# A feed-forward kernel whose next tile's token blocks are prepared at an even pace over a tile's quartets, in a fixed order behind TensorE's products

## The chip, the cores and the metric

One Trainium2 chip, one core. The metric is the device time of one execution in microseconds (us). Engines: PE is TensorE (matrix products), DVE is VectorE, ACT is ScalarE, POOL is GpSimd, SP issues the transfers (DMA).

## What is computed

Attention with 32 landmarks (Nyström) over 4 batches of 576 tokens, and behind it two feed-forward networks over all 2304 tokens (model width 512, inner width 2048). The change lies in the second network. Cut to that:

```python
x = attn_out.transpose(0, 2, 1, 3).reshape(B * S, H * D)      # 2304 x 512
x = _moe_ref(x, w_in, w_out)                                  # first network: x1d in the kernel
h = x @ w_in                                                  # second: 512 -> 2048
g = np.where(h > 0.0, h, np.exp(np.minimum(h, 0.0)) - 1.0)    # ELU
return (g @ w_out).astype(np.float32)                         # 2048 -> 512
```

## The kernel before

The first network leaves its result in DRAM as `x1d`. The second one works on three tiles of 768 tokens (`NTT = 3`), and for each of them on eight quartets (`NQ = 8`) of 256 inner columns. I count the quartets of a tile from 0 to 7. All products are made three times over pairs of numbers, a high part `h` and a low part `l` that together hold a float32 (`wh*xh + wh*xl + wl*xh`).

`quartet(q)` makes the 2x2 block product of weights and tokens by a scheme with seven block products in place of eight (Winograd's form of Strassen's). Each of the seven is a `block`: six matmuls of 128x384 (`h<-x,wi` in the trace) into one of two PSUM banks `h`. So a block can start when the block before the last one has been emptied: the first by ACT's copy `a<-h` (`a1` in the code), the second by DVE's addition `u<-h,a`, the third by `y<-h,a`, and so on. ELU follows on DVE and ACT (`gf<-y`, `gf<-gf,y`), and the result is split into a pair: ACT casts it (`gh<-gf`, `ghl<-gf`), and DVE subtracts (`gl<-gf,gh`, `ghl<-gf,ghl`). Between the blocks PE makes the products of the second layer of an earlier quartet (`x<-w,gh` and the like).

The seven blocks need seven token blocks and seven weight blocks, which are sums of the plain ones:

- `load_in2(q + 1)` loads the next quartet's weights during quartet `q` (`wi<-wi2d`, `u<-wi2d`). In the first tile DVE makes eight additions of 128x128 for them (`u<-u,wi`, `u<-wi,u`), ACT casts (`wi<-wi`, `wi<-u`), POOL subtracts (`wi<-wi`, `wi<-u,wi`), and SP stores the result (`wi2p<-wi`). The two later tiles only load what was stored.
- `load_out2(q)` splits the second layer's weights in the first tile: ACT casts and POOL subtracts (`w<-w`, 128x512).
- `load_x(t, eng)` makes the token blocks of tile `t`, in two halves. A half has four loads from `x1d` (into `xf`, the scratch tiles `f`, and into `x`, the blocks' own places), four subtractions on POOL (`xf<-...`) and seven pairs: a cast on ACT (`x<-x`, `x<-xf`) and a subtraction on POOL. It is a generator: one `next` makes one step, 24 steps for a tile, and a 25th ends it.

For the second and third tile the loop over `q` and `p` (the seven blocks of a quartet) takes one step ahead of each block, from quartet 4 of the tile before (`XPACE = 4`) on:

```python
        if q % NQ == XPACE and q // NQ + 1 < NTT:
            xs = load_x(q // NQ + 1, pool)
...
            gate[0] = chain[0]
            next(xs, None)
            gate[0] = None
```

A scheduler decides the order of instructions in each engine's queue. `wanted(s)` sets their priority, and `after(inst, other)` an order that costs no wait on the chip: `inst` is put in its queue only when `other` has been put in its own. `chain[0]` is the last product written so far. `gated(inst)` puts an instruction behind `gate[0]`. Before, only the loads of `load_x` were gated; subtractions and casts went wherever the scheduler saw room. Once the order is set, each engine works through its own queue in that order and waits only for the data of the instruction at its head.

Of the kernel before, what the change touches and what calls it, by code (L numbers as in the profile page):

```python
# [10 lines left out]
F32 = mybir.dt.float32  # L11
# [20 lines left out]
def nystrom_ffn_kernel(ctx: ExitStack, tc, q, k, v, w_in1, w_out1, w_in2, w_out2, out):  # L32
# [56 lines left out]
    NQ = NKT // 2  # L89
    NTT = NT // (2 * T2)  # L90
# [9 lines left out]
    PRE, NLEAD, EI, EO = 2, 2, 3, 4  # L100
    GATE1, O2, NEW1 = 8, 2, 0
    PACE, NEW, PACE1 = 0.5, -4, 0.2
    XSET, XPACE = 4, 4
    NAT = 25, 28, 31

    strict = [False]
# [17 lines left out]
    def after(inst, other):  # L124

        tc.add_manual_dep(
            inst.ins, other.name, mybir.DependencyInfo(mybir.DependencyClass.NoSync, mybir.DependencyReason.DATA)
        )

    vec, act, pool, pe = InOrder(nc.vector), InOrder(nc.scalar), InOrder(nc.gpsimd), InOrder(nc.tensor)  # L130
    sp = InOrder(nc.sync, False)

    def sub(o, a, b, eng=vec):
        return eng.tensor_tensor(out=o, in0=a, in1=b, op=ALU.subtract)
# [22 lines left out]
    def wanted(s):  # L157
        tc.cur_priority = int(1000 * (s + 100))
# [11 lines left out]
    def gated(inst):  # L170
        if gate[0] is not None:
            after(inst, gate[0])
# [77 lines left out]
    def run(gen):  # L250
        for _ in gen:
            pass
# [55 lines left out]
    def to_pair(f, h, l, eng=vec):  # L308
        act.copy(out=h, in_=f)
        sub(l, f, h.bitcast(F32), eng)  # L310
# [54 lines left out]
    def scratch(n, w):  # L365

        return room().bitcast(F32).rearrange("p n t -> p (n t)")[:, 0:n * w].rearrange("p (a n) -> p a n", a=n)
# [609 lines left out]
    xt_t = {}  # L977

    def x_places(t, n=14):

        for i in range(n):
            if t % 2 == 0:
                x = xp[0].tile([128, 2, T2], F32, name="x2", tag=f"x2{i}")
                yield x[:, 0], x[:, 1]
            elif NS + i < len(PLACES):
                x = wop.tile([128, 2, DM], F32, name="x2", tag=PLACES[NS + i])
                yield x[:, 0, 0:T2], x[:, 1, 0:T2]
            else:
                x = nat.tile([128, G, W], F32, name="x2", tag="nl3")
                yield x[:, 0, 0:T2], x[:, 1, 0:T2]  # L990

    def load_x(t, eng):

        places = x_places(t)
        t0 = 2 * T2 * t
        for kk in range(2):
            x = [next(places) for _ in range(7)]
            h, l = [y[0] for y in x], [y[1] for y in x]

            def pair(i, f):  # L1000
                xt_t[t, kk, i] = h[i].bitcast(F32R), l[i].bitcast(F32R)
                to_pair(f, *xt_t[t, kk, i], eng)

            if t:
                f = [
                    nat.tile([128, G, HALF], F32, name="xf", tag=n).rearrange("p g t -> p (g t)")[:, 0:T2]
                    for n in ("ath0", "ath1", "atl0")
                ]
            else:
                f = scratch(2, T2)  # L1010
                f = [f[:, 0], f[:, 1], scratch(1, T2)[:, 0]]
            for o, r, c in ((f[0], 0, 1), (l[0], 0, 0), (l[2], 1, 1), (l[1], 1, 0)):
                gated(sp.dma_start(out=o, in_=x1d[2 * r + kk, :, t0 + c * T2:t0 + c * T2 + T2]))
            yield
            sub(f[1], f[0], l[0], eng)
            yield
            sub(f[0], l[2], f[0], eng)
            yield
            sub(f[2], l[2], f[1], eng)
            yield  # L1020
            pair(5, f[0])
            yield
            sub(f[0], l[1], f[2], eng)
            yield
            for i, g in ((3, f[1]), (4, f[2]), (6, f[0]), (0, l[0]), (1, l[1]), (2, l[2])):
                pair(i, g)
                yield
# [3 lines left out]
    def bmm(*a):  # L1031

        inst = mm(*a)
        if chain[0] is not None:
            after(inst, chain[0])
        chain[0] = inst.ins
# [12 lines left out]
    def elu(key, src, add, gf=None, split=True):  # L1049

        if gf is None:
            gf = ft.tile([128, T2], F32, name="gf", tag="gf", bufs=2)
        c = stg.tile([128, W], F32, name="y", tag="y", bufs=YB)[:, 0:T2]
        vec.tensor_tensor(out=c, in0=src, in1=add, op=ALU.add)
        act.activation(out=gf, in_=c, func=AF.Relu, scale=-1.0)
        act.activation(out=gf, in_=gf, func=AF.Exp, scale=-1.0)
        vec.scalar_tensor_tensor(out=gf, in0=gf, scalar=-1.0, in1=c, op0=ALU.add, op1=ALU.max)
        if split:
            gt[key] = g_pair()
            to_pair(gf, *gt[key])  # L1060
        return gf
# [4 lines left out]
    def sum_places(t):  # L1066

        places = [y for x in x_places(t + 1, NDEF * NQ // 2) for y in x]
        for r in range(NQ):
            for j in range(NDEF):  # L1070
                sums_t[t * NQ + r, j] = places[NDEF * r + j]

    def quartet(q):

        t = q // NQ
        a1 = nat.tile([128, G, HALF], F32, name="a1", tag="atl1").rearrange("p g t -> p (g t)")[:, 0:T2]
        u2 = scratch(1, T2)[:, 0]
        u3 = ft.tile([128, T2], F32, name="u3", tag="at", bufs=1)

        def block(w, x):  # L1080
            ps = banks["h"].tile([128, 512], F32, name="h", tag="h")[:, 0:T2]
            n = 0
            for kk in range(2):
                wh, wl = wi[q, kk]
                xh, xl = xt_t[t, kk, x]
                for a, b in ((wh, xh), (wh, xl), (wl, xh)):
                    bmm(ps, a[:, w, :], b, n == 0, n == 5)
                    n += 1
            return ps

        def add(o, ps, x):
            vec.tensor_tensor(out=o, in0=ps, in1=x, op=ALU.add)

        act.copy(out=a1, in_=block(0, 0))
        yield
        add(u2, block(5, 4), a1)
        yield
        wino = t in WINO
        if wino:
            if q % NQ == 0:  # L1100
                sum_places(t)
            f = scratch(2, T2)
            f22, f11 = f[:, 0], f[:, 1]
            s1, s2, s3 = (sums_t[q, j] for j in range(NDEF))
        else:
            f22 = f11 = None
        elu((q, 0, 0), block(1, 1), a1, f22)
        yield
        add(u3, block(3, 5), u2)
        yield  # L1110
        ps = block(4, 3)
        elu((q, 1, 1), ps, u3, f11)
        add(u2, ps, u2)
        yield
        f = elu((q, 1, 0), block(2, 6), u3, None, not wino)
        if wino:
            pool.tensor_tensor(out=s1, in0=f22, in1=f, op=ALU.add)
            sub(s2, s1, f11, pool)
            sub(s3, f11, f, pool)
        yield  # L1120
        f = elu((q, 0, 1), block(6, 2), u2)
        if wino:
            sub(f, f, s2)
            gt[q, 4] = g_pair()
            to_pair(f, *gt[q, 4])
        yield
# [283 lines left out]
    for i in range(END, NA):  # L1410
# [3 lines left out]
        if r == 0:  # L1414
# [4 lines left out]
            else:  # L1419
# [3 lines left out]
                x0 = load_x(0, vec)  # L1423
# [19 lines left out]
    def late():  # L1443

        for i in range(NA - DELAY, NA):
            a2 = slot_a2(i, bmm)
            for _ in range(NDM):
                next(a2)
                yield
            run(a2)  # L1450

    def seconds():
        for q in range(NTT * NQ):
            yield from (wino2 if q // NQ in WINO else second)(q)
# [1 line left out]
    flush()  # L1456
    wanted(NA - 6)
    load_in2(1)
    behind, tail, xs, more, n = seconds(), late(), x0, iter(()), 0
    for q in range(NTT * NQ):  # L1460
        wanted(NA + 4 * q - 2)
        if q:
            load_in2(q + 1) if q + 1 < NTT * NQ else None
        if q % NQ == XPACE and q // NQ + 1 < NTT:
            xs = load_x(q // NQ + 1, pool)
        steps_ = quartet(q)
        if q == (WINO[0] - 1) * NQ:
            more = (None for r in range(NQ) for _ in sums_out2(r))
        for p in range(7):
            if p == 2:  # L1470
                load_out2(q)
            wanted(NA + 4 * q + 4 * p / 7 + 4)
            if conv and p % 2 == 0:
                conv.pop(0)()
            if p == 4 and q % NQ == NQ - 2 and q // NQ in WINO:
                load_late2(q // NQ, 0)
                load_late2(q // NQ, 1)
            next(more, None)
            gate[0] = chain[0]
            next(xs, None)  # L1480
            gate[0] = None
            wanted(NA + 4 * q + 4 * p / 7)
            next(steps_)
            for _ in range(2):
                next(tail, None)
            while n < (7 * q + p + 1 - 7 - LAG) * 12 * NS2 // 7:
                next(behind)
                n += 1
        run(steps_)
# [37 lines left out]
```

## Time and profile before

| | |
|---|---|
| median of 3 runs | 826.49 us (822.29 to 826.56) |
| profiled execution | 825.29 us, span 823.5 us, mean granted clock 0.991 |
| PE busy | 783.3 us, 95% of the span |
| DVE, ACT, POOL busy | 545.6, 463.7, 413.2 us |
| second network | from 431.68 us (first `h<-x,wi`) to the end |

Busy times are of one execution. Since PE is busy nearly all the time, a wait of another engine matters only where PE waits for it in turn. Tiles are named without numbers: `x` is a token block (or, as a matmul's output, a PSUM bank), `u` scratch, `w` weights of the second layer.

### The profile page before, as it was taken

The page shows a single profiled execution, that of the slowest core. Times are in us where ns is not written, and L with a number is a line of the kernel's source. Part 1 is how long each engine was busy: PE and PEld are TensorE (multiplying, and loading weights), DVE is VectorE, ACT ScalarE, POOL GpSimd, SP SyncE. Part 2 cuts the span into 40 slices and gives each one's busy share as a digit, 9 for nine tenths or more (in the row PEclk, how much of TensorE's full clock was granted, in tenths as well). Part 3 has the DMA queues.
Part 4 walks back from the last instruction along what each step waited for, and adds up shares of the span by engine and source line. Part 5 has one row for each costly group of instructions (what it writes and reads, how often), then busy time and mean ns, then how long its engine had stood idle before and what let it go on. Part 6 is the DMA issues. An engine that isn't in the chain of part 4 may idle for free.

```text
span 823.5 us, 16234 instructions
## 1 busy us (share of the span) xinstructions
PE 783.3 (95%) x5860; PEld 694.7 (84%) x5860; DVE 545.6 (66%) x1076; ACT 463.7 (56%) x1020; POOL 413.2 (50%) x423
## 2 busy tenths in 40 slices
PE   5699999999999999999999998979999999999998
PEld 3476777687997889889998897869989889999998
DVE  6898677557645754486346768776756645777795
ACT  3687454656556656574545556645644644555562
POOL 2566566557655665455412448859734560133311
PEclk9799999999999999999999999999999999999999
DMA  9966932675578545752332675778999667777663
GB/s 318 404 186 230 314 112 85 185 259 198 190 231 263 166 142 162 239 192 100 131 129 87 224 272 193 256 263 306 377 388 363 213 225 265 258 247 264 216 200 111
DMA packets 115600, 184.57 MB, mean 224 GB/s; under 512 B 8576, under 2 KB 71552, under 8 KB 115520
## 3 DMA queue, kind: packets, MB, share of 16 engines
q1 hardware_dynamic: 115520, 183.54, 65.4%
q8 instruction: 46, 0.75, 0.4%
q14 instruction: 34, 0.28, 0.1%
HBM read 130.02 MB, written 53.48 MB: 223 GB/s over the span
## 4 chain that ended last, share of the span: by engine, by line
PE 64%; DVE 15%; DMA 10%; ACT 5%; issue 3%; POOL 2%; SPq 1%; DVEq 0%; ACTq 0%; POOLq 0%
PE x L116 33%; PE h L116 26%; PE bk L116 5%; DVE u L116 3%; DMA u<-in_moe_w_in 2%; DMA u<-in_moe_w_out 2%; DVE h L116 2%; DMA wi<-wi2d 1%; DVE gf L116 1%; DVE nl L116 1%; DVE w1c L116 1%; DMA kt<-in_k 1%; DVE y L116 1%; DMA x<-x1d 1%; ACT gf L116 1%
## 5 line engine op out<-in xcount | busy, mean ns | idle before, releaser
L116 PE MATMUL h<-x,wi 128*128 128x384 f32 x1008 | 205.4, 339 | 8.4 <-DVE u L116 6.4
L116 PE MATMUL x<-gh,wo 128*128 128x288 f32 (+1 forms) x896 | 199.0, 297 | 0.6 <-DVE wo L116 0.3
L116 PEld LDWEIGHTS h<-x,wi 128*128 128x128 f32 x1008 | 178.2, 189 | 19.8 <-DVE u L116 8.2
L116 PEld LDWEIGHTS x<-gh,wo 128*128 128x128 f32 x896 | 149.3, 188 | 10.8 <-issue 7.2
L116 PE MATMUL x<-gl,wo 128*128 128x288 f32 (+1 forms) x448 | 130.6, 293 | 0.0
L116 POOL TENSOR_TENSOR gl<-gf,gh 128x288 fp32r<-128x288 f32 (+1 forms) x100 | 83.7, 839 | 86.8 <-ACT gh L116 75.9
L116 ACT CAST gh<-gf 128x288 fp32r<-128x288 f32 (+2 forms) x160 | 72.5, 454 | 85.4 <-DVE gf L116 85.1
L116 PE MATMUL x<-w,gh 128*128 128x512 f32 (+1 forms) x360 | 102.2, 357 | 0.1
L116 DVE SCALAR_TENSOR_TENSOR gf<-gf,y 128x384 f32<-128x384 f32 x80 | 65.5, 819 | 35.8 <-ACT gf L116 35.6
L116 ACT ACTIVATE gf<-h,half_b 128x288 f32<-128x288 f32 (+2 forms) x128 | 63.8, 500 | 43.9 <-PE h L116 42.0
L116 PE MATMUL h<-atl,nh 128*128 128x288 f32 (+2 forms) x256 | 81.7, 319 | 6.7 <-DVE gf L116 3.2
L116 DVE SCALAR_TENSOR_TENSOR gf<-gf,h 128x288 f32<-128x288 f32 (+1 forms) x112 | 49.4, 442 | 55.3 <-ACT gf L116 54.6
L116 PEld LDWEIGHTS x<-gl,wo 128*128 128x128 f32 x448 | 84.2, 188 | 1.1 <-issue 0.9
L116 PE MATMUL x<-w,ghl 128*128 128x512 f32 (+1 forms) x324 | 77.2, 358 | 0.1
L116 PE MATMUL h<-ath,nl 128*128 128x288 f32 (+2 forms) x256 | 76.5, 299 | 0.0
L116 PE MATMUL h<-ath,nh 128*128 128x288 f32 (+2 forms) x256 | 76.3, 298 | 0.0
L116 ACT ACTIVATE gf<-y 128x384 f32<-128x384 f32 x80 | 41.9, 524 | 54.4 <-DVE y L116 54.2
L116 PEld LDWEIGHTS x<-w,gh 128*128 128x128 f32 x360 | 65.0, 189 | 6.5 <-ACT gh L116 0.5
L116 PEld LDWEIGHTS h<-atl,nh 128*128 128x128 f32 x256 | 48.4, 189 | 20.1 <-DVE gf L116 7.3
L116 PE MATMUL x<-w,gl 128*128 128x512 f32 (+1 forms) x180 | 64.5, 358 | 0.7 <-DVE gl L116 0.7
L116 POOL TENSOR_TENSOR x<-u,gf 128x384 f32<-128x384 f32 x16 | 18.1, 1152 | 86.2 <-DVE gf L116 50.9
L116 PEld LDWEIGHTS x<-w,ghl 128*128 128x128 f32 x324 | 55.5, 190 | 5.9 <-DVE ghl L116 0.3
(183 smaller groups left out, 1519.8 us busy)
## 6 DMA issues: line engine op xcount, KB each, us to landing
wi<-wi2p SPq DMA_DIRECT2D x64, 448.0 KB, 5.9
wi2p<-wi SPq DMA_DIRECT2D x32, 448.0 KB, 2.7
u<-in_moe_w_in SPq DMA_DIRECT2D x25, 512.0 KB, 4.5
w1c<-w1d SPq DMA_DIRECT2D x48, 256.0 KB, 4.5
w<-wo2p SPq DMA_DIRECT2D x24, 512.0 KB, 7.4
ub<-in_moe_w_out SPq DMA_DIRECT2D x16, 512.0 KB, 10.2
u<-in_moe_w_out SPq DMA_DIRECT2D x16, 512.0 KB, 5.7
wo2p<-w SPq DMA_DIRECT2D x16, 512.0 KB, 3.9
```

Of the source, the lines that this page charges most:

```text
L116: inst = getattr(self.eng, name)(*a, **kw)
```

## The change

The steps of `load_x` for the second tile start in quartet 1 of the first tile, at block 9 (7 times the quartet and the block within it), and are dealt out evenly up to block 54, the 25 calls over 45 blocks. For the third tile they run from block 28 to 54 of the second one. Subtractions and casts are gated as the loads are, each behind the products written so far at its place. (For the first tile `gate[0]` is empty, so nothing is gated there, and its steps were all made before the loop already.)

```diff
-    XSET, XPACE = 4, 4
+    XSET, XFROM, XTO, XSTEPS = 4, (9, 28, 99), 54, 25
...
             def pair(i, f):
                 xt_t[t, kk, i] = h[i].bitcast(F32R), l[i].bitcast(F32R)
-                to_pair(f, *xt_t[t, kk, i], eng)
+                gated(act.copy(out=xt_t[t, kk, i][0], in_=f))
+                gated(sub(xt_t[t, kk, i][1], f, xt_t[t, kk, i][0].bitcast(F32), eng))
...
             yield
-            sub(f[1], f[0], l[0], eng)
+            gated(sub(f[1], f[0], l[0], eng))
             yield
-            sub(f[0], l[2], f[0], eng)
+            gated(sub(f[0], l[2], f[0], eng))
             yield
-            sub(f[2], l[2], f[1], eng)
+            gated(sub(f[2], l[2], f[1], eng))
             yield
             pair(5, f[0])
             yield
-            sub(f[0], l[1], f[2], eng)
+            gated(sub(f[0], l[1], f[2], eng))
...
-    behind, tail, xs, more, n = seconds(), late(), x0, iter(()), 0
+    run(x0)
+    behind, tail, xs, more, n, xn = seconds(), late(), iter(()), iter(()), 0, 0
...
-        if q % NQ == XPACE and q // NQ + 1 < NTT:
+        if q % NQ == 1 and q // NQ + 1 < NTT:
             xs = load_x(q // NQ + 1, pool)
+            xn = 0
...
             gate[0] = chain[0]
-            next(xs, None)
+            at = 7 * (q % NQ) + p - XFROM[q // NQ]
+            while xn < min(at * XSTEPS // (XTO - XFROM[q // NQ]), XSTEPS):
+                next(xs, None)
+                xn += 1
             gate[0] = None
```

Where the instructions go is seen in the queues. On PE nothing moves. POOL's queue in the first tile, between two pairs of weight splits (the pair `w_6374`, `w_6378` stands at the end of quartet 3's work, `w_6558` in quartet 4), before the change; `xf` and `x_65..` are the second tile's token blocks, `wi` the next quartet's weights:

```order
L116 TENSOR_TENSOR w_6378<-w_6378 128x512
L116 TENSOR_TENSOR xf<-xf,x_6513 128x384
L116 TENSOR_TENSOR xf<-x_6515,xf 128x384 x2
L116 TENSOR_TENSOR x_6513<-x_6513 128x384
L116 TENSOR_TENSOR x_6516<-xf,x_6516 128x384
L116 TENSOR_TENSOR wi<-wi 128x384
L116 TENSOR_TENSOR x_6515<-x_6515 128x384
L116 TENSOR_TENSOR x_6518<-xf,x_6518 128x384
L116 TENSOR_TENSOR wi<-wi 128x384
L116 TENSOR_TENSOR wi<-u,wi 128x512
L116 TENSOR_TENSOR x_6517<-xf,x_6517 128x384
L116 TENSOR_TENSOR wi<-u,wi 128x512
```

The same stretch of POOL's queue with the change, the splits of quartet 2 (`w_6222`) up to those of quartet 3 (`w_6396`); the names are numbered anew:

```order
L116 TENSOR_TENSOR w_6222<-w_6222 128x512
L116 TENSOR_TENSOR x_6078<-xf,x_6078 128x384
L116 TENSOR_TENSOR xf<-x_6074,xf 128x384
L116 TENSOR_TENSOR x_6076<-xf,x_6076 128x384
L116 TENSOR_TENSOR wi<-wi 128x384 x2
L116 TENSOR_TENSOR wi<-u,wi 128x512
L116 TENSOR_TENSOR x_6077<-xf,x_6077 128x384
L116 TENSOR_TENSOR wi<-u,wi 128x512
L116 TENSOR_TENSOR w_6396<-w_6396 128x512
```

Eight token instructions stood between two pairs of splits, five of them ahead of the first `wi`; now four do, three ahead of the first `wi`. Over the whole tile the groups between pairs were of 8, 3, 9 and 2, and are of 3, 4, 4, 3, 4 and 4.

ACT's queue at the end of quartet 3 before the change (`a_6527<-h` is the first copy of quartet 4, `ghl<-gf` the cast of an ELU result, `x_65..` casts of token blocks):

```order
L116 ACTIVATE gf<-gf 128x384
L116 CAST x_6513<-x_6513 128x384
L116 CAST ghl<-gf 128x384
L116 CAST x_6515<-x_6515 128x384
L116 ACTIVATE gf<-y 128x384
L116 CAST x_6516<-xf 128x384
L116 CAST x_6514<-x_6514 128x384
L116 CAST wi<-wi 128x384
L116 ACTIVATE gf<-gf 128x384
L116 COPY a_6527<-h 128x384
```

And the same place with the change, where `a_6541` is that copy:

```order
L116 ACTIVATE gf<-gf 128x384
L116 CAST x_6074<-x_6074 128x384
L116 CAST ghl<-gf 128x384
L116 ACTIVATE gf<-y 128x384
L116 CAST wi<-wi 128x384
L116 ACTIVATE gf<-gf 128x384
L116 CAST wi<-wi 128x384
L116 COPY a_6541<-h 128x384
L116 CAST wi<-u 128x512
```

Four casts of token blocks stood here, the first of them right behind the block's load; one is left, of a block loaded two quartets earlier.

SP's queue in quartet 3 before the change, from the stores of the splits to the loads of the next weights `wi<-wi2d`:

```order
L116 DMA wo2p<-w_6378 128x2x512
L116 DMA xf<-x1d 128x384
L116 DMA x_6513<-x1d 128x384
L116 DMA x_6515<-x1d 128x384
L116 DMA x_6514<-x1d 128x384
L116 DMA wi<-wi2d 128x384 x2
```

SP's queue in quartet 1 with the change:

```order
L116 DMA wi2p<-wi 128x896
L116 DMA xf<-x1d 128x384
L116 DMA wi2p<-wi 128x896
L116 DMA u<-wi2d 128x128
L116 DMA wi2p<-wi 128x896
L116 DMA x_6073<-x1d 128x384
L116 DMA x_6075<-x1d 128x384
L116 DMA x_6074<-x1d 128x384
L116 DMA u<-wi2d 128x128
L116 DMA wi2p<-wi 128x896
L116 DMA wi<-wi2d 128x384 x2
```

The four loads of the first half moved up two quartets, and among the stores of the weights; those of the second half moved up one quartet, to the same places in SP's queue as before, ahead of `wi<-wi2d`.

## Rows read from the trace of the kernel before

**Rows 1.** The page: busy time, share of the span and instructions.

```profile
PE 783.3 (95%) x5860; PEld 694.7 (84%) x5860; DVE 545.6 (66%) x1076; ACT 463.7 (56%) x1020; POOL 413.2 (50%) x423
```

**Rows 2.** Waits of PE from 425 us: total, times, longest.

```profile
PE h L116 <- DVE u L116: 6.4, 3, 2.7
```

**Rows 3.** Windows: quartets 2 to 6, then the second tile; clock, DMA share, GB/s last.

```profile
459.40:475.40 16.00, 15.94 (x79) 14.09 (x78) 11.07 (x24) 9.55 (x19) 8.27 (x6) 1.00 0.68 244
475.40:491.06 15.66, 15.66 (x80) 14.12 (x79) 11.73 (x25) 9.42 (x19) 8.26 (x6) 1.00 0.75 262
491.06:512.32 21.26, 17.76 (x80) 15.28 (x78) 15.42 (x23) 12.26 (x26) 18.68 (x16) 0.92 0.54 193
512.32:527.95 15.63, 15.63 (x80) 14.12 (x78) 11.33 (x23) 9.79 (x22) 11.00 (x10) 1.00 0.82 282
527.95:549.22 21.27, 16.48 (x79) 13.93 (x78) 17.28 (x23) 11.52 (x25) 17.93 (x16) 1.00 0.61 223
...
564.90:690.75 125.85, 125.85 (x626) 113.31 (x624) 76.62 (x126) 67.95 (x139) 68.52 (x65) 1.00 0.87 306
```

**Rows 4.** Windows: POOL's instructions on `x` alone; whole stretch, then quartets 4, 6, 5.

```profile
487.00:550.00 63.00, 24.70 (x22) 0.97 0.67 237
...
491.06:512.32 21.26, 10.85 (x10) 0.92 0.54 193
527.95:549.22 21.27, 10.48 (x10) 1.00 0.61 223
512.32:527.95 15.63, 3.37 (x4) 1.00 0.82 282
```

**Rows 5.** Timeline of ACT: start, us, operation, idle before and releaser.

```profile
492.79 0.52 ACT L116 CAST x<-x 128x384 fp32r<-128x384 f32 x1 [3.06 <-DMA x<-x1d]
...
525.84 0.51 ACT L116 CAST x<-x 128x384 fp32r<-128x384 f32 x1 [1.27 <-DMA x<-x1d]
```

**Rows 6.** Groups of DVE in quartets 3, 4 and 6: busy us, mean ns.

```profile
L116 DVE TENSOR_TENSOR u<-u,wi 128x128 f32<-128x128 f32 x4 | 1.1, 288 | 0.2 <-DMA wi<-wi2d 0.2
...
L116 DVE TENSOR_TENSOR u<-u,wi 128x128 f32<-128x128 f32 x4 | 3.0, 744 | 0.5 <-DMA wi<-wi2d 0.4
...
L116 DVE TENSOR_TENSOR u<-u,wi 128x128 f32<-128x128 f32 x4 | 3.8, 947 | 0.0
```

**Rows 7.** Timeline of DVE and of PE in quartets 2, 3 and 4.

```profile
465.87 0.55 DVE L116 TENSOR_TENSOR u<-h,a 128x384 f32<-128x384 f32 x1
...
466.47 1.33 PE L116 MATMUL h<-x,wi 128*128 128x384 f32 x6
...
480.52 0.54 DVE L116 TENSOR_TENSOR u<-h,a 128x384 f32<-128x384 f32 x1
...
482.25 1.21 PE L116 MATMUL h<-x,wi 128*128 128x384 f32 x6
...
493.75 0.58 DVE L116 TENSOR_TENSOR ghl<-gf,ghl 128x384 fp32r<-128x384 f32 x1 [2.96 <-ACT ghl L116]
...
501.23 0.54 DVE L116 TENSOR_TENSOR u<-h,a 128x384 f32<-128x384 f32 x1
...
501.83 1.91 PE L116 MATMUL h<-x,wi 128*128 128x384 f32 x6 [2.72 <-DVE u L116]
```

**Rows 8.** Timeline of SP's issues in quartets 1 and 3.

```profile
453.89 0.46 SPq L116 DMA_DIRECT2D wi2p<-wi  x1
457.92 0.84 SPq L116 DMA_DIRECT2D wi<-wi2d  x2
...
488.46 2.21 SPq L116 DMA_DIRECT2D x<-x1d  x3
490.77 0.85 SPq L116 DMA_DIRECT2D wi<-wi2d  x2
```

**Rows 9.** Timeline of POOL: its last token instruction in the second tile.

```profile
678.04 1.38 POOL L116 TENSOR_TENSOR x<-xf,x 128x384 fp32r<-128x384 f32 x1
```

## The prediction

> **What bounds the kernel now.** I read the page first: PE is busy for 95% of the span [rows 1], so time comes back only where PE stands. The waits of PE from 425 us to the end, the second feed-forward network, are above all for one thing: a `u` written by VectorE (DVE), 6.4 us in three waits [rows 2]. To see where, I cut the first tile into its quartets at the first product of each (459.40, 475.40, 491.06, 512.32, 527.95 and 549.22 us) and asked for busy times in these windows [rows 3]. A quartet in which PE never waits takes 15.66 us (quartet 3) or 15.63 (quartet 5). Quartets 4 and 6 take 21.26 and 21.27 with the same 79 or 80 products. That is the loss in question: 21.26 + 21.27 - 15.66 - 15.63 = 11.24 us. It holds PE's waits and what follows them: the granted clock of quartet 4 is 0.92, and the six products after its longest wait take 1.91 us instead of 1.21 [rows 3, 7].
>
> What sets these two quartets apart is the next tile's token blocks, the work that the change moves. Of its 22 instructions on GpSimd (POOL), 24.70 us, ten run in quartet 4 and ten in quartet 6, and four in quartet 5 (an instruction across an edge counts twice) [rows 4]. Two things happen there.
>
> First, ScalarE (ACT) stands at a cast of a token block whose transfer hasn't landed, 3.06 us in quartet 4 and 1.27 just before quartet 6 [rows 5]. Behind that cast in ACT's queue is the cast `ghl<-gf`, so DVE gets its `ghl` 2.96 us late, at 493.75 [rows 7].
>
> Second, DVE's eight additions for the next weights (`u<-u,wi` and `u<-wi,u`, 128x128) run while POOL works. The four of one kind take 288 ns each in quartet 3, 744 in quartet 4 and 947 in quartet 6 [rows 6]. Behind them in DVE's queue is `u<-h,a`, which empties the bank that PE's fourth block of the quartet needs. In quartet 3 it ends at 480.52 + 0.54 = 481.06, and PE starts that block at 482.25: 1.19 us to spare. In quartet 4 it ends at 501.77, and PE starts at 501.83 after 2.72 us of waiting [rows 7].
>
> **The change part by part.** It adds and removes no instruction; PE's own order is the same. Three edits matter.
>
> *The steps are spread over quartets 1 to 7 instead of 4 to 7, and each stands behind PE's products.* Between pairs of weight splits (`w_... 128x512`) POOL's queue had groups of 8, 3, 9 and 2 token instructions; now it has 3, 4, 4, 3, 4 and 4. On ACT, no cast of a block stands ahead of a cast that PE needs until its transfer has had several blocks of PE to land in. So both causes go from quartets 4 and 6: -11.24 us.
>
> *What the spread load costs elsewhere.* Each of six quartets now carries 24.70/6 = 4.1 us of POOL work. Lower bound: nothing. Quartet 5 carried 3.37 us of it and took 15.63 us, the shortest of all [rows 3, 4]. Upper bound: DVE's busy time was 15.42 and 17.28 us in the two crowded quartets against 11.73 in quartet 3, which is 3.69 and 5.55 us for 10.85 and 10.48 us of POOL work, 0.34 to 0.53 us for each [rows 3, 4]. At 0.53 a quartet loses 4.1 x 0.53 = 2.2 us on DVE, and less 1.19 us of slack about 1.0. The nearest row is quartet 5, and the groups now mostly follow the weight splits, behind DVE's additions and not ahead of them; for quartets 3, 4 and 6 I take 0.1 us each, 0.3 in all.
>
> *The four loads of each half move in SP's queue.* In quartet 3 the loads of the first half stood right ahead of the weight loads `wi<-wi2d`: three of them take 2.21 us to issue, so four take about 2.95, and the weights were issued at 490.77, the moment SP was free [rows 8]. The clean distance is that from 457.92 to 459.40, 1.48 us ahead of a quartet's first product; 490.77 is only 0.29 ahead of 491.06, so 1.2 us late. In the new place, in quartet 1, SP is idle from 454.35 to 457.92, 3.57 us [rows 8], which covers 2.95. If it didn't, the cost would be direct, because quartet 2 has nothing to spare: its `u<-h,a` ends at 466.42 and PE takes the block at 466.47 [rows 7]. Bounds 0 and 2.95; I take 0.8, nearer the end that SP's idle time supports, and a part for the three subtractions that now fall there. The second half's loads go into quartet 4 and meet quartet 5, with 1.19 us of slack: bounds 0 and 1.8, I take 0.5.
>
> *The second tile* (28 to 54 in place of 28 on, now behind PE) is worth nothing: PE is busy for 125.85 of 125.85 us from the second tile's first product to the third's [rows 3]. Its last POOL step ends at 679.42 [rows 9], 11.3 us ahead of the third tile's first product at 690.75; two blocks of PE later (some 4.5 us) is still ahead. Without that cover each late us would be one us.
>
> **Sum.** 825.29 (the profiled execution) - 11.24 + 0.3 + 0.8 + 0.5 = 815.7 us. That execution is 1.2 us under the median of the three runs, 826.49, and 3.0 above the lowest, 822.29; on the median's scale it is 816.9. I forecast 816.5.
>
> **The rivals.** Half a per cent, 4.1 us, is about what a measurement of this kernel can tell from no change.
>
> *The spread load costs every quartet.* At the upper bound above, six quartets lose 1.0 us each: 825.3 - 11.2 + 6 = 820.1, on the median's scale 821. For it speaks DVE's 0.53 us for each of POOL in quartet 6, against it quartet 5.
>
> *The stalls move with the transfers.* Quartets 2 and 5, which now stand behind the loads, lose the 5.6 us that 4 and 6 lost: 825.3, no change. For it: quartet 2 has no slack. Against it: no cast of ACT now waits for these loads, and SP has 3.57 us to spare. With it goes the case that the order does nothing, since nothing but place in a queue holds a step back, and the steps slide together again: also 825.
>
> *Slower.* Every us of POOL's work is passed on whole: a POOL instruction keeps DVE from SBUF until it ends. Then each of six quartets loses 4.1 - 1.19 = 2.9 us on DVE's additions, 17.6 in all: 831.6. It decides from (11.24 + 4.1)/6 = 2.6 us a quartet. Against it: the crowded quartets passed on 0.34 to 0.53, and `u<-h,a`, which reads PSUM, takes 0.54 us in quartets 3 and 4 alike [rows 7]. The Trainium skill states such a rule (SBUF — State Buffer, Who interferes with whom): a DVE instruction with two SBUF inputs and a GpSimd instruction that reads SBUF share a port pair that is locked for the whole instruction, and the loser blocks fully. By that rule only two-SBUF additions such as `u<-u,wi` lengthen, and the trace agrees: 288 ns become 744 to 947 there, while the one that reads PSUM doesn't change.
>
> **How the numbers follow.** Stalls gone, little in their place (814 to 818.5): 0.57. Every quartet pays (818.5 to 822.5): 0.20, four fifths of it under the bound of 0.5% (822.4). Stalls move, or nothing changes (823 to 828): 0.17. Slower: 0.06. So faster 0.57 + 0.16 = 0.73, same 0.21, slower 0.06. The range starts at 811.5, near the lowest run less the whole 11.24 us (811.05), and ends at 823.5, past the second case; what lies beyond is the last two cases, about 0.2.
>
> **What would show it.** Right: quartets 4 and 6 at 15.6 to 16.5 us; `u<-u,wi` near 300 ns in both; no wait of ACT over 1 us for a token transfer; PE's waits for `u` in the first tile under 2 us; quartet 2 longer by at most 1 us; the second tile still without a wait. Wrong: a wait of PE for `u` or for ACT's `a` in quartets 2, 3 or 5 of over 2 us; weights `wi<-wi2d` issued later than 1 us ahead of a quartet's first product; POOL's token instructions in the same stretch as the 128x128 additions again.

## The result, and the profile after

| | before | after |
|---|---|---|
| median | 824.63 us (822.28 to 826.56, 7 runs) | 816.82 us (814.51 to 820.2, 7 runs) |
| ratio | | 0.9911, 95% interval 0.9884 to 0.9939 |
| profiled execution, span | 825.29, 823.5 us | 814.51, 812.7 us |
| second network starts (first `h<-x,wi`) | 431.68 us | 429.70 us |
| from there to the end of the span | 391.8 us | 383.0 us |
| quartets 2 to 7 of the first tile together | 105.45 us | 95.34 us |

The kernel became 0.9% faster; 816.5 was forecast. Of the 10.8 us between the two spans, 2.0 lie ahead of the second network, whose start differs from one execution of the same kernel to the next (the changed kernel, profiled once more as e5, has it at 431.17). The change can be read in the second network alone, and there it is worth 8.8 us, or 7.5 by the second profile (384.3 us from there to the end).

The page of the changed kernel, busy time and the chain of work that ended last (to be read beside [rows 1]):

```profile
PE 781.7 (96%) x5860; PEld 693.6 (85%) x5860; DVE 539.0 (66%) x1076; ACT 463.4 (57%) x1020; POOL 415.7 (51%) x423
...
PE 73%; DMA 9%; DVE 7%; ACT 4%; POOL 3%; issue 2%; SPq 0%; DVEq 0%; POOLq 0%; ACTq 0%
```

Waits of PE from 425 us in the changed kernel (us in total, times, longest), against the 6.4 us in three waits of [rows 2]:

```profile
PE h L116 <- DVE u L116: 0.8, 2, 0.6
PE x L116 <- DVE gl L116: 0.7, 1, 0.7
PE h L116 <- ACT a L116: 0.5, 2, 0.3
```

Windows of the changed kernel: quartets 2 to 7, the second tile's first quartet, and the rest of that tile. The columns are those of [rows 3]: length, busy time of PE, PEld, DVE, ACT and POOL, granted clock, DMA share, GB/s:

```profile
457.44:473.36 15.92, 15.92 (x80) 13.98 (x78) 11.73 (x23) 9.72 (x21) 12.26 (x10) 1.00 0.62 228
473.36:488.99 15.63, 15.63 (x80) 14.12 (x78) 12.56 (x24) 11.28 (x25) 13.41 (x11) 1.00 0.74 262
488.99:504.66 15.67, 15.67 (x80) 14.23 (x78) 12.74 (x24) 9.88 (x21) 13.18 (x11) 1.00 0.78 274
504.66:520.29 15.63, 15.63 (x79) 14.12 (x78) 11.67 (x24) 9.94 (x20) 10.67 (x8) 1.00 0.69 249
520.29:536.66 16.37, 16.06 (x79) 14.00 (x78) 12.11 (x23) 10.44 (x22) 13.23 (x12) 1.00 0.66 242
536.66:552.78 16.12, 15.90 (x79) 14.04 (x78) 10.30 (x16) 8.25 (x18) 9.78 (x10) 1.00 0.92 326
552.78:569.78 17.00, 16.24 (x80) 13.99 (x79) 11.10 (x18) 11.05 (x23) 16.30 (x16) 1.00 1.03 367
569.78:679.96 110.18, 110.18 (x548) 99.16 (x547) 65.32 (x111) 57.09 (x118) 52.64 (x51) 1.00 0.83 294
```

Quartet 4 went from 21.26 to 15.67 us, and its mean granted clock from 0.92 to 1.00; quartet 6 went from 21.27 only to 16.37. The quartets that follow the moved loads, 2 and 5, did not lengthen. But two stretches that had been clean now aren't: quartet 7 (15.64 before, 16.12 now) and the second tile's first quartet (15.71 before, 17.00 now). Where these 2.5 us come from (0.73 in quartet 6, 0.48 and 1.29 there) was the open question.

The token work on POOL stands in every quartet now. Windows of the changed kernel, POOL's instructions on `x` alone, quartets 3, 4 and 6 (compare [rows 4]):

```profile
473.36:488.99 15.63, 5.23 (x5) 1.00 0.74 262
488.99:504.66 15.67, 5.00 (x5) 1.00 0.78 274
...
520.29:536.66 16.37, 5.27 (x6) 1.00 0.66 242
```

And the additions on DVE in the same three quartets (count, busy us, mean ns), against 288, 744 and 947 ns in [rows 6]:

```profile
L116 DVE TENSOR_TENSOR u<-u,wi 128x128 f32<-128x128 f32 x4 | 1.1, 286 | 0.1
...
L116 DVE TENSOR_TENSOR u<-u,wi 128x128 f32<-128x128 f32 x4 | 1.0, 278 | 0.0
...
L116 DVE TENSOR_TENSOR u<-u,wi 128x128 f32<-128x128 f32 x4 | 1.9, 494 | 1.2 <-DMA wi<-wi2d 1.2
```

Five us of POOL's work in quartets 3 and 4 leave these additions at their undisturbed time: in quartet 4 POOL idles from 490.62 to 492.69 us, and the additions start at 490.96. In quartet 6 they wait for the weights' transfer. ACT has no wait for a token transfer left in quartets 2 to 7, where [rows 5] showed 3.06 and 1.27 us.

### The profile page after: what moved, and what is told of

Read it like the earlier page. It is cut to its first block, busy times and chain, and to the rows that moved or that the text cites. A ratio compares the mean times of both kernels' runs of the same rounds, so it can differ in the third digit from the quotient of the medians.

```text
span 812.7 us, 16236 instructions
## 1 busy us (share of the span) xinstructions
PE 781.7 (96%) x5860; PEld 693.6 (85%) x5860; DVE 539.0 (66%) x1076; ACT 463.4 (57%) x1020; POOL 415.7 (51%) x423
## 4 chain that ended last, share of the span: by engine, by line
PE 73%; DMA 9%; DVE 7%; ACT 4%; POOL 3%; issue 2%; SPq 0%; DVEq 0%; POOLq 0%; ACTq 0%
PE x L116 38%; PE h L116 29%; PE bk L116 6%; DMA u<-in_moe_w_out 3%; DMA u<-in_moe_w_in 2%; DVE u L116 1%; DMA wi<-wi2d 1%; DMA kt<-in_k 1%; DMA w<-wo2d 1%; DVE gf L116 1%; POOL x L116 1%; DVE lm L116 1%; DVE st L116 1%; DVE x L116 1%; ACT nh L116 1%
## 5 line engine op out<-in xcount | busy, mean ns | idle before, releaser
L116 DVE SCALAR_TENSOR_TENSOR gf<-gf,y 128x384 f32<-128x384 f32 x80 | 67.4, 842 | 34.2 <-ACT gf L116 34.2
```

What stands on the lines that cost most here:

```text
L116: inst = getattr(self.eng, name)(*a, **kw)
```

## The experiments

Each kernel is the changed one with the edit shown, except where said. Unless a row is named, quartet lengths are taken as in the windows above, from first product to first product, in one profile of each kernel. A ratio is taken within a series, over all runs of both kernels, and isn't exactly the quotient of the medians; the kernel before had medians of 824.63 us (beside after), 824.86 (e1 to e4), 826.45 (e5 to e8) and 824.93 (e9, e10). e3 and e4 ran once and are read by their quartets alone.

| | median, us (runs) | ratio to before, 95% | quartets 2 to 7 | 2nd tile's first |
|---|---|---|---|---|
| before | 824.63 (7) | | 105.45 | 15.71 |
| after | 816.82 (7) | 0.9911 (0.9884 to 0.9939) | 95.34 | 17.00 |
| e1 order, old pace | 820.53 (10) | 0.996 (0.9943 to 0.9977) | 98.57 | 17.02 |
| e2 pace, no order | 825.32 (10) | 1.0012 (0.9994 to 1.003) | 106.04 | 15.90 |
| e3 bunch at the start | 822.34 (1) | | 101.69 | 15.71 |
| e4 bunch in the middle | 819.41 (1) | | 99.75 | 15.68 |
| e5 after again | 817.35 (4) | 0.9906 (0.9883 to 0.9928) | 96.52 | 17.00 |
| e6 edge ordered | 816.95 (6) | 0.9902 (0.988 to 0.9923) | 96.06 | 15.86 |
| e7 second half later | 815.61 (6) | 0.9878 (0.9852 to 0.9904) | 94.84 | 15.86 |
| e8 subtractions twice | 824.59 (10) | 0.9987 (0.9967 to 1.0007) | 101.84 | 17.43 |
| e10 loads first, alone | 814.82 (5) | 0.9879 (0.9843 to 0.9914) | 94.21 | 16.99 |
| e9 all orders | 813.92 (5) | 0.987 (0.9836 to 0.9903) | 94.55 | 15.87 |

The theory at this point was that of the prediction: two causes, token casts in ACT's queue ahead of casts that PE needs, and POOL's token work beside DVE's additions, both cured by place in the queues. The main rivals were that the pace alone does it, and that the amount of work in one place does it, whatever the order.

### Order and pace apart (e1, e2)

The order with the old pace, one step ahead of each block from quartet 4 on:

```diff
-        if q % NQ == 1 and q // NQ + 1 < NTT:
+        if q % NQ == XPACE and q // NQ + 1 < NTT:
...
-            while xn < min(at * XSTEPS // (XTO - XFROM[q // NQ]), XSTEPS):
-                next(xs, None)
-                xn += 1
+            next(xs, None)
```

> The new order behind PE's products is kept, the even pace is not: the second tile's steps start in quartet 4 again, one for each block, so quartets 4 to 7 carry 22 POOL instructions, 5 or 6 each. If what the change won comes from the order (no cast of ACT ahead of a landed transfer, no bunch of POOL's instructions ahead of DVE's additions), nearly all of it stays: quartets 4 to 7 take 15.6 to 16.6 us each, the six quartets 2 to 7 together 95 to 98 us (105.45 before, 95.34 with the change), 815 to 820 us in all. If the even pace is what counts, quartets 4 to 6 lose 2 us or more each: over 101 us for the six, over 822 in all.

The pace with nothing but the loads ordered:

```diff
-                gated(act.copy(out=xt_t[t, kk, i][0], in_=f))
-                gated(sub(xt_t[t, kk, i][1], f, xt_t[t, kk, i][0].bitcast(F32), eng))
+                to_pair(f, *xt_t[t, kk, i], eng)
...
-            gated(sub(f[1], f[0], l[0], eng))
+            sub(f[1], f[0], l[0], eng)
```

(and so for the other three subtractions).

> The even pace is kept, the order of subtractions and casts is not (only the loads are ordered, as before the change). The queues show two bunches of eight token instructions on POOL again, now ahead of the weights of quartets 2 to 3 and 5 to 6. If the order is what counts, two quartets (2 and 5 in place of 4 and 6) lose 4 to 6 us each: 104 to 107 us for quartets 2 to 7, no faster than before. If spreading alone suffices: 95 to 97 us, 815 to 819 in all.

The order alone kept 6.9 of the 10.1 us that the change gives back in quartets 2 to 7 (of 8.9 by its second profile), a little less than expected; the pace alone kept nothing. Windows of e2, POOL's instructions on `x`, quartets 2 to 5:

```profile
456.08:477.58 21.50, 10.56 (x10) 0.92 0.51 183
477.58:493.21 15.63, 0.00 (x0) 1.00 0.70 254
493.21:508.88 15.67, 0.83 (x1) 1.00 0.81 286
508.88:529.87 20.99, 11.52 (x11) 0.92 0.51 174
```

The steps were written in at an even pace, and still ran in two bunches, right behind their loads, now in quartets 2 and 5, with the same loss of over 5 us each. That is the prediction's second rival (the steps slide together again): it is what the pace does without the order.

In e1 the losses stand in quartets 5 and 6 (17.78 and 17.98 us). Timeline of ACT in e1 (start, us, operation, idle before and releaser):

```profile
508.78 0.51 ACT L116 CAST x<-xf 128x384 fp32r<-128x384 f32 x1 [3.15 <-POOL xf L116]
...
529.20 0.51 ACT L116 CAST wi<-wi 128x384 fp32r<-128x384 f32 x1 [1.56 <-DMA wi<-wi2d]
```

With one step a block, ACT again reaches a cast before its data are there, this time POOL's subtraction; and the second half's loads go out just ahead of the weights' loads, which land late. Order and pace are needed together.

### The two causes apart (e3, e4)

Both keep the order and bunch the steps in the first tile: the loads of each half four blocks (e3) or ten blocks (e4) ahead, and the rest of the half behind one product.

```diff
+    LOAD, START = (24, 38), (28, 42)
...
-            while xn < min(at * XSTEPS // (XTO - XFROM[q // NQ]), XSTEPS):
+            upto = min(at * XSTEPS // (XTO - XFROM[q // NQ]), XSTEPS)
+            if q < NQ:
+                at = 7 * q + p
+                upto = (at >= LOAD[0]) + 11 * (at >= START[0]) + (at >= LOAD[1]) + 12 * (at >= START[1])
+            while xn < upto:
```

> Takes the wait for transfers away and keeps the bunch: each half's loads are put in order four blocks ahead of everything else of that half, and all its casts and subtractions stand behind one product, at the start of quartets 4 and 6, so that POOL's bunch meets DVE's eight additions for the next weights. If both causes count: no wait of ACT over 0.5 us for a token transfer, u additions at 600 ns or more in quartets 4 and 6, and these lose 2 to 4 us each, 100 to 103 us for quartets 2 to 7. If the wait of ACT for the transfer was the whole cause: under 97. If POOL's bunch was the whole cause: 105 or more.

In e4 `LOAD, START` are `(21, 35), (31, 45)`: the first bunch stands behind block 3 of quartet 4, behind the additions.

> The same two bunches, but behind a product of block 3 of quartets 4 and 6, after DVE's eight additions. If the loss comes from the place (POOL's work on top of the additions, at the quartet's start), quartets 4 and 6 take 15.6 to 16.8 us though each carries 10 or 11 token instructions: 95 to 98 us for quartets 2 to 7. If it comes from the amount of POOL's work in one quartet (0.34 to 0.53 us of DVE for each of POOL), they lose 2.5 to 4.5 us each wherever it stands: 100 to 104.

In e3 ACT has no wait for a token transfer any more, so one cause is gone. What is left is in the groups of DVE (the additions in quartet 4) and, below it, the timeline of PE:

```profile
L117 DVE TENSOR_TENSOR u<-u,wi 128x128 f32<-128x128 f32 x4 | 2.8, 691 | 0.7 <-DMA wi<-wi2d 0.6
```

```profile
501.40 2.16 PE L117 MATMUL h<-x,wi 128*128 128x384 f32 x6 [2.88 <-DVE u L117]
...
537.05 1.32 PE L117 MATMUL h<-x,wi 128*128 128x384 f32 x6 [2.53 <-DVE u L117]
```

The additions beside the bunch still take 691 ns, and the two quartets lose 4.7 and 2.8 us of the 11.24: the second cause alone. Their waits are nearly alike; what differs is TensorE's granted clock behind them (window of each quartet):

```profile
491.53:511.88 20.35, 17.47 (x79) 15.44 (x78) 16.70 (x25) 10.41 (x23) 15.81 (x14) 0.92 0.55 198
527.51:545.97 18.46, 15.93 (x80) 14.06 (x78) 15.29 (x22) 9.49 (x21) 15.47 (x14) 1.00 0.59 211
```

In the 2.6 us behind the wait of 2.88 us the granted clock was 0.53, near the lower of its two levels (1.2 and 2.4 GHz), and the six products took 2.16 us; behind the wait of 2.53 us it stayed at 1.00, and they took 1.32. So some of the loss in quartet 4 is the clock.

That the other 3.8 us were the first cause doesn't follow from e3 by itself, since its bunch is also smaller (8.11 us of POOL's token work in quartet 4, 10.85 before). e4 shows that cause at work: quartet 4 lost 2.2 us there although its additions were undisturbed. ACT, DVE, PE and the additions in e4's quartet 4:

```profile
502.91 0.51 ACT L117 CAST x<-xf 128x384 fp32r<-128x384 f32 x1 [0.78 <-POOL xf L117]
503.33 0.51 ACT L117 CAST gh<-gf 128x384 fp32r<-128x384 f32 x1
...
503.87 1.65 DVE L117 TENSOR_TENSOR gl<-gf,gh 128x384 fp32r<-128x384 f32 x1 [1.87 <-ACT gh L117]
...
506.51 1.32 PE L117 MATMUL h<-x,wi 128*128 128x384 f32 x6 [1.61 <-DVE u L117]
...
L117 DVE TENSOR_TENSOR u<-u,wi 128x128 f32<-128x128 f32 x4 | 1.1, 288 | 1.1 <-DMA wi<-wi2d 1.1
```

ACT stands at token casts that wait for POOL, with a cast that DVE needs behind them, so that DVE stands for 1.87 us. That is the first cause with another releaser. (`gl<-gf,gh` beside POOL, 1.65 us where it took 0.71 in quartet 3 of the changed kernel, adds to it; how the 3.8 us divide no run shows.) e4 lost another 2.6 us in quartet 5 and 0.7 in quartet 3: in both the weights went out at the quartet's very start (0.06 us behind it, and 0.06 ahead), and in quartet 5 POOL was still working the bunch off when the additions came. At 99.75 e4 fell between the two expectations.

### The amount (e8)

```diff
-                gated(sub(xt_t[t, kk, i][1], f, xt_t[t, kk, i][0].bitcast(F32), eng))
+                for _ in range(2 if t else 1):
+                    gated(sub(xt_t[t, kk, i][1], f, xt_t[t, kk, i][0].bitcast(F32), eng))
```

> As the changed kernel, but each of the 14 pairs of a tile's token blocks has its subtraction on POOL made twice, the second writing the same values to the same place: some 15 us more of POOL work over quartets 2 to 7, in the same order. Theory that place decides and the amount is covered: quartets 2 to 7 together 95.3 to 98 us, time up by 0 to 3 us. Rival, every quartet pays 0.53 us on DVE for each us of POOL beyond 1.19 of slack: 6.7 x 0.53 - 1.19 = 2.4 us in each of six quartets, 14 us, together about 108 and the time 828 to 832. In between, up by 4 to 10 us: there is cover for the load as it is, but not for much more, and the forecast of 0.1 us a quartet was near an edge.

(For three of the seven pairs of a half, block and result share a place, so that there the second subtraction takes the high part off once more and leaves another low part; the work is the same.) Quartets 2 to 7 took 101.84 us: 5.3 to 6.5 more than in the two profiles of the changed kernel, the case in between. POOL's work on `x` in e8 and the group of additions, both in quartet 4 (18.47 us), and what PE waits for there:

```profile
492.10:510.57 18.47, 9.46 (x9) 1.00 0.65 221
```

```profile
L116 DVE TENSOR_TENSOR u<-u,wi 128x128 f32<-128x128 f32 x4 | 4.3, 1102 | 0.0
```

```profile
501.62 1.33 PE L116 MATMUL h<-x,wi 128*128 128x384 f32 x6 [2.52 <-DVE u L116]
```

POOL can't finish between two sets of additions any more, and its backlog lies beside them: 1102 ns for one instead of 278. So the even load is free only up to a point, and that point isn't far: making the pairs' subtractions twice takes away most of the gain (5.3 to 6.5 of the 8.9 to 10.1 us in these quartets).

### What the change lost on the way (e5, e6, e7, e10, e9)

e5 is the changed kernel again.

> The changed kernel once more, unaltered, to stand beside the next ones. Expected 815 to 818 us, ratio to before 0.990 to 0.992; in its profile quartets 2 to 7 of the first tile together 95 to 95.7 us, the first quartet of the second tile about 17.0 (17.00 in the first profile, 15.71 in that of before).

Quartets 2 to 7 took 96.52 us, longer than expected. Most of that is in quartet 6 (17.13 us against 16.37); quartets 3 and 7 took 15.93 and 16.38 us against 15.63 and 16.12. The timelines of the two profiles show why for quartet 6. The changed kernel at the edge of quartets 5 and 6, which starts at 520.29 us: SP, POOL, ACT, PE:

```profile
517.72 1.95 SPq L116 DMA_DIRECT2D wo2p<-w  x2
519.75 1.43 SPq L116 DMA_DIRECT2D wi<-wi2d  x2
...
516.40 2.86 POOL L116 TENSOR_TENSOR w<-w 128x512 fp32r<-128x512 f32 x2
...
523.22 0.51 ACT L116 CAST wi<-wi 128x384 fp32r<-128x384 f32 x1 [1.23 <-DMA wi<-wi2d]
523.64 0.51 ACT L116 CAST x<-xf 128x384 fp32r<-128x384 f32 x1
...
524.88 0.47 ACT L116 COPY a<-h 128x384 f32<-128x384 f32 x1
...
525.40 1.32 PE L116 MATMUL h<-x,wi 128*128 128x384 f32 x6 [0.31 <-ACT a L116]
```

And e5, whose quartet 6 starts at 521.99:

```profile
521.57 1.48 SPq L116 DMA_DIRECT2D wi<-wi2d  x2
...
525.67 0.29 DVE L116 TENSOR_TENSOR u<-u,wi 128x128 f32<-128x128 f32 x1 [1.60 <-DMA wi<-wi2d]
...
527.85 1.32 PE L116 MATMUL h<-x,wi 128*128 128x384 f32 x6 [1.07 <-ACT a L116]
```

Token work on POOL stands ahead of quartet 5's weight splits, which end at 519.26. Their stores wait for them at the head of SP's queue, and the loads `wi<-wi2d` of the weights stand behind the stores. So the loads go out 0.54 and 0.42 us ahead of the quartet instead of 1.48. DVE's additions start on them 2.93 us behind its start (523.22 - 520.29) in one profile and 3.68 in the other, 0.75 later, and the quartet loses 0.73 and 1.49 us, 0.76 more.

e6 puts the casts and subtractions of `sums_out2` (the second layer's weights for the third tile, made from the second tile's start on) behind PE's products, and takes its step there:

```diff
-            to_pair(y, x.bitcast(F32R), y.bitcast(F32R), pool)
+            gated(act.copy(out=x.bitcast(F32R), in_=y))
+            gated(sub(y.bitcast(F32R), y, x, pool))
...
-            next(more, None)
             gate[0] = chain[0]
+            next(more, None)
```

> As the changed kernel, and the casts and subtractions of sums_out2, which run from the end of the first tile on, are put behind PE's products too. With it ACT's order around the edge of the tiles goes back to that of before: the cast ghl<-gf ahead of the cast x<-x 128x512. Theory: the 1.29 us that the second tile's first quartet lost, and most of the 0.48 of quartet 7, come from that x<-x cast, which waits for POOL with ghl<-gf and a<-h behind it. Then that first quartet takes 15.7 to 15.9 and quartet 7 15.6 to 15.9, and the time falls by 1.3 to 1.8 us against the changed kernel. Rival: the loss there comes from the spread token work itself, which now reaches to the tile's end (POOL's w splits late, weights of the next tile late). Then the quartet stays at 16.5 to 17.0 and the time is the changed kernel's.

The cause it was made for, in the timelines of the changed kernel: ACT, DVE and PE in the second tile's first quartet.

```profile
555.40 0.62 ACT L116 CAST x<-x 128x512 fp32r<-128x512 f32 x1 [0.69 <-POOL x L116]
555.93 0.51 ACT L116 CAST ghl<-gf 128x384 fp32r<-128x384 f32 x1
...
557.28 0.46 ACT L116 COPY a<-h 128x384 f32<-128x384 f32 x1
...
556.47 1.27 DVE L116 TENSOR_TENSOR ghl<-gf,ghl 128x384 fp32r<-128x384 f32 x1 [2.40 <-ACT ghl L116]
...
560.84 1.31 PE L116 MATMUL h<-x,wi 128*128 128x384 f32 x6 [0.55 <-DVE u L116]
```

It is the pattern of [rows 5, 7] again, with another family of casts: one that waits for POOL stands ahead of `ghl<-gf` and `a<-h`. Nothing in the diff touches `sums_out2`; its place in ACT's queue changed because the work around it did. In after, e1, e5 and e10 this `ghl<-gf` starts 3.1 us behind the quartet's start, and the quartet takes 16.99 to 17.02 us; in before, e2, e3, e4, e6, e7 and e9 it starts 0.1 to 2.0 us behind it, and the quartet takes 15.68 to 15.90. (In e2 and e3 a cast `x<-x` stands ahead of it as well, but its wait is over earlier: what counts is how late `ghl<-gf` gets. e8, with more work on POOL, is apart: 1.8 and 17.43.) With the order of e6, which has `ghl<-gf` ahead of these casts, it took 15.86, as expected. Quartet 7 did not get shorter (16.66, where 15.6 to 15.9 was expected), so its loss is another, and its cause isn't shown. In it ACT stands at a cast `w<-w` that waits for its transfer `w<-wo2d`, with casts of ELU results behind it: 1.61 us in the changed kernel, 1.87 in e5, 2.13 in e6, while the quartet lost 0.48, 0.74 and 1.02 against the 15.64 of before, where ACT has no such wait. But in e9 and e10 the wait is 1.62 and 1.68 us and the quartet loses only 0.26 and 0.31, so the wait alone doesn't set the loss. The median hardly moved (816.95 against 817.35 in the same series, where 1.3 to 1.8 us were expected).

e7 adds to e6 that the second half's subtractions and casts start at block 37 (`XHALF`), behind quartet 5's splits:

```diff
-            while xn < min(at * XSTEPS // (XTO - XFROM[q // NQ]), XSTEPS):
+            upto = min(at * XSTEPS // (XTO - XFROM[q // NQ]), XSTEPS)
+            if q < NQ and upto > 13:
+                upto = max(13, 13 + (7 * q + p - XHALF) * 12 // (XTO - XHALF))
+            while xn < upto:
```

> As the one before, and the second half's subtractions and casts start at block 37 (behind quartet 5's w splits) instead of block 33, so that no token subtraction stands in POOL's queue ahead of quartet 5's first w split. Theory: the 0.73 us that quartet 6 lost is a chain over queues: token work ahead of the w splits on POOL, their stores late in SP's queue, the loads wi<-wi2d behind the stores issued only 0.54 us ahead of the quartet's first product, DVE and ACT waiting for them. Then these loads go out 1.2 us or more ahead, and quartet 6 takes 15.6 to 15.8; the time falls by 0.3 to 0.7 us more, if the denser steps in quartets 6 and 7 cost nothing. Rival: the loss is that of additions u<-u,wi beside POOL (place of the load); then quartet 6 stays at 16.2 or above and the loss moves with the steps to quartets 6 and 7.

Quartet 6 got shorter (16.11) but not clean, and the step that was to do it failed: a token subtraction got between the two splits, and the loads went out at 518.10, 0.35 us ahead of the quartet's start at 518.45. A token cast no longer stood between `wi<-wi` and `a<-h` on ACT, which may be what helped. So the late loads were still to be tested by themselves. e10 is the changed kernel with one order more, on SP:

```diff
-            sp.dma_start(out=flat[1][:, 0:3 * 128], in_=wi2d[q, kk][:, 0:3 * 128])
+            ld = sp.dma_start(out=flat[1][:, 0:3 * 128], in_=wi2d[q, kk][:, 0:3 * 128])
             if kk:
                 for o, i in stores:
-                    sp.dma_start(out=o, in_=i)
+                    st = sp.dma_start(out=o, in_=i)
+                    if q > 1 and o.shape[1] == 2:
+                        after(st, ld.ins)
```

> The changed kernel, and one more order in SP's queue: in the first tile the stores wo2p<-w stand behind the next quartet's weight loads wi<-wi2d instead of ahead of them. No token instruction is moved: the cast x<-xf stays between wi<-wi and a<-h on ACT, and POOL's token work stays ahead of the w splits. In two profiles of the changed kernel these loads went out 0.54 and 0.42 us ahead of quartet 6's first product, landed 2.93 and 3.68 us behind it, and the quartet lost 0.73 and 1.49 us. Theory: quartet 6 loses because the loads are late in SP's queue. Then they go out 1.2 to 1.5 us ahead and quartet 6 takes 15.6 to 15.8 us; the tile's edge keeps its loss (17.0 us in the second tile's first quartet). Time 0.7 to 1.5 us below the changed kernel's. Rival: it loses because of the token cast in ACT's queue or POOL's work itself; then it stays at 16.3 or above.

Timeline of SP in e10, at the edge of quartet 6, and below it the windows of quartets 6, 7 and the second tile's first:

```profile
522.03 0.85 SPq L116 DMA_DIRECT2D wi<-wi2d  x2
522.97 0.90 SPq L116 DMA_DIRECT2D wo2p<-w  x2
```

```profile
523.52:539.18 15.66, 15.66 (x79) 14.23 (x78) 12.17 (x24) 11.18 (x24) 12.25 (x10) 1.00 0.78 292
539.18:555.13 15.95, 15.91 (x79) 14.05 (x78) 10.01 (x15) 7.82 (x17) 9.30 (x10) 1.00 0.90 317
555.13:572.12 16.99, 16.25 (x79) 14.00 (x78) 11.11 (x18) 11.05 (x23) 16.38 (x16) 1.00 1.03 364
```

The loads go out 1.49 us ahead, and quartets 2 to 6 all take 15.64 to 15.66 us, with the token work where the change put it. So quartet 6 doesn't lose by the token cast or POOL's work themselves: it was the stores in SP's queue, and the cast can cost something only while the loads are late. The median, 814.82 us, fits, but its interval (0.9843 to 0.9914) overlaps with that of the changed kernel. The tile's edge keeps its loss, as expected.

e9 takes all of it together: e7 and the order of e10.

> All orders together: the changed kernel, the casts and subtractions of sums_out2 behind PE's products, the second half's token steps from block 37 on, and the stores wo2p<-w behind the weight loads wi<-wi2d in the first tile. If the three losses found (quartet 6, quartet 7, the edge of the tiles) have these causes, quartets 2 to 7 take 15.6 to 15.9 us each (together 94 to 94.7), the second tile's first quartet 15.9, and from quartet 2's first product to the end of the span it is 353 to 353.8 us, against 355.3 and 356.4 in two profiles of the changed kernel. Time 2 to 3 us below the changed kernel's. Rival: the stores, now behind the loads, hold up the loads w<-wo2d that follow them in SP's queue, and the w splits get late: PE waits at a product x<-w of over 1 us, and the gain is lost again.

Quartets 3 to 6 took 15.63 to 15.67 us, quartet 7 15.90, the second tile's first 15.87; quartet 2 took 16.05, where its weights landed 2.80 us behind its start, against 1.86 in e10 (15.66). From quartet 2's first product to the end it is 353.7 us, as expected, against 355.3 and 356.4 for the changed kernel and 364.1 before. The stores behind the loads cost no wait of PE for `w`. The median, 813.92 us, is the lowest of all kernels here; its interval (0.9836 to 0.9903) overlaps with that of the changed kernel in the series of e5 (0.9883 to 0.9928), so that e9 is faster than the changed kernel is shown by the quartets, in one profile against two, not by the times.

## Why the prediction was right, term by term

The mechanism was the predicted one. On the profiled scale -9.64 us was predicted, and the second network measured -8.8, or -7.5 by the second profile. That 816.82 lies so near to 816.5 is in part luck: the forecast started from a median of 826.49, which more runs brought down to 824.63, so that the medians differ by 7.8 us and not by 10. And in the sum two errors partly cancel: the loads and the spread load were charged 1.6 us and cost nothing in the first profile, while quartets 6 and 7 and the tile's edge kept 2.5 us that were put at nothing. (The edge of quartet 3 was read as 475.40; its product starts at 475.42, and the loss in question is 11.26.)

- **Quartets 4 and 6, -11.24.** Quartet 4 gave back 5.59 us, all of its stall. Quartet 6 gave back 4.90, or 4.14 in the second profile. Both causes named were real: e3 shows the additions beside POOL without the wait for transfers, e4's quartet 4 the casts on ACT with undisturbed additions, and e2 brought the loss back in other quartets. What the term left out is a third queue: SP's stores ahead of the weights. It had named the sign for it, weights issued later than 1 us ahead of a quartet, and that came true in quartet 6 (0.54 and 0.42 us).
- **Spread load, +0.3.** Right in its smallness: quartets 3 and 4 took 15.63 and 15.67. DVE's busy time did rise, from 11.73 us to 12.56 and 12.74, 0.16 to 0.20 us for each us of POOL's token work, and the slack took it up: in quartet 3 `u<-h,a` ends at 479.71 and PE takes its bank at 480.18, 0.47 us to spare instead of 1.19. In the second profile that was too little: the additions of quartet 3 waited 0.36 and 0.25 us for their weights, and it took 15.93 us. The 0.73 us in quartet 6 look like this term, and aren't: e10 removes them by the order of the stores on SP.
- **Loads, +0.8 in quartet 2 and +0.5 in quartet 5.** Mis-sized: -0.09 and 0.00 (-0.23 and 0.00 in the second profile). In quartet 1 the four loads ended 3.4 us ahead of the weights, which went out at 455.95, 1.49 us ahead of quartet 2, the clean distance. Covered by the idle SP that the prediction had named.
- **"The second tile is worth nothing", 0.** This step failed in its first quartet: +1.29, and +0.48 in quartet 7 just ahead of it. The prediction looked at the token steps of the second tile and their cover, not at what else changes its place in a queue when they leave. e6, which orders these casts, takes the 1.29 us down to 0.15; the 0.48 stay open. The side effect on `sums_out2` could have been seen in ACT's order before any run.

Of the rivals, *every quartet pays* was wrong: quartets 2 to 6 are clean in e10 under the same load. *The stalls move* is what e2 does; the order prevents it. *Slower* by a whole instruction's lock had its mechanism right and its reach wrong. A 128x128 addition took 1102 ns in e8 beside POOL instructions of 1.1 to 1.3 us that follow each other without a gap, and 278 in the gap of POOL, while `u<-h,a`, which reads PSUM, took 0.55 us in either. That agrees with the Trainium skill (SBUF — State Buffer, Who interferes with whom), by which a DVE instruction with two SBUF inputs and a GpSimd instruction that reads SBUF exclude each other, and the later one waits for the whole of the other. But it costs time only where the two meet, and the change keeps POOL's token work away from the additions. With the work that e8 adds it no longer fits between them, and the median is 7.2 us higher (824.59 against 817.35).

Open: what quartet 7 loses, and why the transfer `w<-wo2d` lands later in it than before the change (no run took that wait away); and what makes the weights' landing scatter in quartets 2 and 3 (15.66 to 16.05 and 15.63 to 15.93 us for them).

## What to carry to other kernels

Spreading side work evenly in the program does nothing if the scheduler may pull it together again (e2); an order behind the main engine's products is what holds it in place, and both are needed (e1). Put in-order queues in the sequence in which the bottleneck needs their results: a cast that waits for a transfer, and a store that waits for a late result, each block what is queued behind them (ACT in [rows 5], SP in e10). When work leaves a stretch, read the queues of that stretch again for what moved up in its place, since the order of untouched work can change too.

## What was not expected of the hardware

The same pair of loads `wi<-wi2d`, issued at the same place in SP's queue, took 3.47 us from issue to DVE's start in one profile of the changed kernel and 4.10 in the other. With the loads 0.5 us ahead of need that scatter goes straight into the time (16.37 and 17.13 us for one quartet). With 1.48 us ahead it shows less, but it shows: in the second profile DVE waits for the weights of quartet 3, which take 4.16 us from issue to its first addition, and the quartet takes 15.93 us instead of 15.63:

```profile
477.44 0.29 DVE L116 TENSOR_TENSOR u<-u,wi 128x128 f32<-128x128 f32 x1 [0.36 <-DMA wi<-wi2d]
```
